# An attention and SwiGLU kernel: new delays between the steps that finish a phase's outputs, a later load of values, and the last projection tile moved among the closing steps

## The chip, the cores and the metric

The kernel runs on one core of a Trainium2 chip. The core has five engines, each with its own queue of instructions that it works through in order: PE multiplies matrices, DVE does vector work, ACT does exponentials and copies, POOL does slower vector work, and SP here only issues transfers (DMAs). Engines wait for each other through semaphores. The metric is device microseconds (us) of one execution, the median of several runs.

## What is computed

The input x has 2048 tokens of width 512. After a layer norm it goes through two branches, both in float32:

```python
xn = _layernorm(x, axis=-1)
qkv = xn @ wqkv                       # 32 heads of 16
p = softmax(q @ k.T * 16 ** -0.5)     # 2048 x 2048 per head
s = concat(p @ v) @ wo
g = silu((silu(xn @ w1) * (xn @ w3)) @ w2)   # inner width 1792
return x + s * g
```

## The kernel before, in words

**Products.** A float32 matrix is split into a high and a low part (`hi`, `lo`), and a product is three matmuls (`split3`, lines 187, 189 and 191; in the feed-forward branch line 814).

**Phases.** Attention goes by 32 phases: 16 pairs of heads, each with two halves of the queries. For a phase, PE makes scores keys by queries (`scores`, line 587, tile `e`), ACT exponentiates them (line 590, tile `pt`), and PE multiplies the result with the values (`values`, line 600, tile `pv`), in 16 steps over the keys, each called a V step below and numbered through the kernel from 0 to 511. The score matmul also subtracts a maximum of each query's row, which rides along as two extra rows of `qs`. These maxima come from a second pass of scores, queries by keys (`max_unit`, line 380, tile `m`), reduced by DVE (line 382, tile `mp`). When a phase's maxima are complete, `max_rows` works in three stages: DVE reduces and negates (lines 388 and 390), PE transposes and DVE splits into `mh` and `ml` (394 to 398), and SP issues four transfers that write the rows into `qs` (line 405). The next phase's `e` matmuls wait for them.

**A phase's outputs.** After a phase's last V step, `take_out` copies `pv` to `ot` at once (ACT, line 606) and then goes on in six steps, called *sums* (4 transfers of the softmax's sums, line 612), *reciprocal* (DVE, 614), *rd* (1 transfer of the reciprocals to memory, 616), *rb* (4 transfers that read them back spread over rows, 619), *multiply* (DVE 621, then the split `oh`, `ol` on POOL, 624 and 625), and *out* (8 transfers, 633). The list `outs` holds the phases whose steps are still to come.

**What orders the work.** Nothing is decided on the chip. A planner in the Python code keeps a clock (`mod.now`) that it advances by fixed costs, and emits instructions as it goes; each engine then runs its own in that order. A long string, `ORDER_OF_ISSUE`, says what PE gets next: s and S are score matmuls of one half of the array's rows, m and M maxima, f and F the feed-forward branch, v a V step, r and R the middle stage of `max_rows`, o a tile of the output projection, a dot a pause. Before every character the planner calls `settle`, `small` (which takes the steps of `max_rows` and `take_out` that are due), `tend` (transfers of the last part, `tasks`) and `catch_up` (characters that could not be served when they came, the list `late`; it serves several o's in a row with no call of `small` between them).

In `small`, before, each output step is due a fixed time of the planner's clock after the last: 7.0, and 4.0 for phases from 27 on:

```python
if c[0] <= mod.now:
    c[0] = mod.now + (7.0 if c[2] < PHASES - 5 else 4.0)
```

**The last part.** `steps` lists 22 pieces of the output projection. A piece ("whole", b, t), called tile (b, t) below, is 12 matmuls, for a block b of 512 tokens and t of its four 128-token tiles; blocks go in the order 3, 2, 0, then the rest of block 2, then 1. `finish` multiplies by the gate, adds x (lines 983 and 984) and stores. Tiles (0, t) and (1, t) need the outputs of phase 30, which `taken_out(PHASES - 2)` asks for; its *out* step writes straight into the tiles `ov` that they read (k = 3 of each product, the last three of 12 matmuls). When block 2's tiles are issued, `tend` issues eight loads for block 1 (lines 914 and 915, 256 KB each) into the space that block 2 frees; those of block 0 go the same way before. Phase 31 ends with a closing stretch of its own (lines 1226 to 1245): ACT copies `pv` (1227), the remaining tiles are run, `shares` sums with PE and takes reciprocals (1032 to 1035), `turn_back` transposes (1041), DVE multiplies (1238), ACT and DVE split (1240, 1241), and four last products follow.

Of the kernel before, what the change touches and what calls it, by code (L numbers as in the profile page):

```python
# [1 line left out]

# [14 lines left out]
P = 128  # L17
S, D, F = 2048, 512, 1792
H, DH = 32, 16
NP = H // 2  # L20
KC = D // P
# [13 lines left out]
GH = 4  # L35
RING = 9
AHEAD = 5
HALF = P // 2
EARLY = 0.5

# [86 lines left out]
    "svvSmMmsMvSsMmvSffMSfMfSffMfMfSfFfFsFsFmFsFfFmFsFfMsFfFmFsFfMfSfFsFmMfFfSfFfSmFfFmFsSfFmSvvvmSmSsFFs"  # L129
    "FmFFsFmFFsmFmFFsFmFmFsFFmFsFmFsSvSmFsmFsSvvsSsSsSvvmSSsSsvvmSsSsSSvmSsSSvvMsSsSsMvMsMsMsvMsMsMsS...."  # L130
    "..oSssSSrSovSssSSsSovvSssSSsosSsSSsvvsSsSSovsSSsSovSsSsSovSsSvvvoooooSssSSsosSvsSsSosSvvSsoooooosSSs"
    "SsosSsSSsovsvsvvv..."
)


def raw(ap):
    return ap.bitcast(F32)
# [3 lines left out]
def kernel(ctx: ExitStack, tc: tile.TileContext, x, wqkv, wo, w1, w3, w2, out):  # L141
    nc = tc.nc
# [14 lines left out]
    def take(v):  # L157

        i = min(range(BANKS), key=lambda i: (free_at[i], taken_at[i]))
        uses[i] += 1  # L160
        kind[i] = v
        was_free[i] = free_at[i]
        taken_at[i] = sum(uses)
        free_at[i] = max(t for t in free_at if t < 1e8) + 0.001
        return i, psum.tile([P, 512], F32, tag=f"bank{i}", name=v, bufs=1)

    def bank(v):
        return take(v)[1]
# [16 lines left out]
    def split3(ps, lhs, rhs, first, last):  # L185

        nc.tensor.matmul(ps, lhs[1], rhs[0], start=first, stop=False)  # L187
        yield
        nc.tensor.matmul(ps, lhs[0], rhs[1], start=False, stop=False)  # L189
        yield  # L190
        nc.tensor.matmul(ps, lhs[0], rhs[0], start=False, stop=last)  # L191
        yield

    def run(gen):
        for _ in gen:
            pass
# [90 lines left out]
    mod = Model()  # L287
# [120 lines left out]
    with tc.tile_pool(name="pro", bufs=1) as pro:  # L408
# [24 lines left out]
        half = pro.tile([P, 1], F32, name="half")  # L433
# [88 lines left out]
        for b in range(TB):  # L522
# [4 lines left out]
            for i, u in enumerate((2, 3, 0, 1) if b == 0 else (2, 0, 1, 3)):  # L527
                t = b * 4 + i

                for v in range(2):  # L530
                    rbk = u * 2 + v
                    ps = bank("e")
# [26 lines left out]
                r = next(blank, None)  # L559
# [84 lines left out]
    def settle():  # L644
        wts.fill()
        for e in list(owed):
            if e in owed and e[0] <= max(mod.now, mod.free[e[1]] if e[1] in mod.free else 0) + 0.1:
                owed.remove(e)
                e[3](e[0])
# [188 lines left out]
    ov, wos, side, sums, there = {}, [], {}, [], {}  # L838
# [113 lines left out]
    def tend():  # L952

        while tasks and not any(c[2] for c in rows) and mod.free["dma"] <= mod.now + 3.0:
            e = next((e for e in tasks if e[1]()), None)
            if e is None:
                return
            tasks.remove(e)
            e[2]()
            if e[3]:  # L960
                there[e[0]] = mod.work("dma", mod.now, e[3]) + 2.5
# [5 lines left out]
    steps = [("whole", b, t) for b in (3, 2, 0) for t in range(4)]  # L967
# [11 lines left out]
    def finish(b, t, i, ps, to, adder=None):  # L979

        xr, gr = side[b, t]
        res = tail.tile([P, 512], F32, tag="res", name="res", bufs=2) if adder is None else pt_tile(F32)
        nc.vector.scalar_tensor_tensor(res, gr, 0.25, ps, op0=ALU.mult, op1=ALU.mult)
        (adder or nc.vector).tensor_add(xr, res, xr)
        free_at[i] = mod.work("dve", max(mod.lane) + 0.25, 1.4) - 0.7
        if to is not None:
            r = b * 512 + t * P
            to.dma_start(out[r:r + P, :], xr)

    def pt_tile(dtype):  # L990
        return work.tile([P, 512], dtype, tag="pt", name="pt", bufs=PTS)

    def projecting():

        if not steps or min(free_at) > mod.now + EARLY or not can(*steps[0][:2]):
            return False
        what, b, t = steps.pop(0)
        i, ps = take("o")
        if what == "sum":
            mod.block(3, was_free[i])  # L1000
            side["spread"] = shares(sums[0], ps, tail.tile([P, 512], F32, tag="res", name="res", bufs=2))
            free_at[i] = mod.work("dve", max(mod.lane) + 0.25, 0.8) - 0.5
            sums.append(free_at[i] + 0.8)
            return True
        if what == "back":
            mod.block(4, was_free[i])
            ot = sums[0]
            turn_back(ps, side["spread"])
            oh, ol = (work.tile([P, 512], F32R, tag=f"o{v}", name=f"o{v}", bufs=1) for v in "hl")
            nc.vector.tensor_mul(ot, ot, ps)  # L1010
            nc.vector.tensor_scalar(oh, ot, 1.0, 1.0, op0=ALU.mult, op1=ALU.mult)
            nc.vector.tensor_sub(ol, ot, raw(oh))
            free_at[i] = mod.work("dve", max(mod.lane) + 0.25, 2.0) - 1.2
            sums.append(free_at[i] + 1.5)
            side["split"] = oh, ol
            return True
        if what == "whole":
            mod.block(3 * KC, was_free[i])
            for k in range(KC):
                run(split3(ps, [v[k][:, t * P:(t + 1) * P] for v in ov[b]], [w[k] for w in wos], k == 0, k == KC - 1))  # L1020
        else:
            mod.block(3, was_free[i])
            run(split3(ps, [v[:, t * P:(t + 1) * P] for v in side["split"]], wlast, True, True))
        finish(b, t, i, ps, nc.sync if b < TB // 2 or what == "last" else None)
        return True
# [3 lines left out]
    def shares(ot, ps, spread):  # L1029

        for c in range(4):
            nc.tensor.matmul(ps[:, 4 * c:4 * c + 4], ot[:, c * P:(c + 1) * P], picks[0], start=True, stop=True)
        rec = work.tile([P, 16], F32, tag="rec", name="rec", bufs=2)
        nc.vector.reciprocal(rec, ps[:, 0:16])
        nc.vector.tensor_copy(spread.rearrange("p (a b) -> p a b", b=32),
                              rec.rearrange("p (a b) -> p a b", b=1).to_broadcast([P, 16, 32]))
        return spread

    def turn_back(ps, spread):
        for c in range(4):  # L1040
            nc.tensor.transpose(ps[:, c * P:(c + 1) * P], spread[:, c * P:(c + 1) * P], ident)
# [66 lines left out]
    def small(due=False):  # L1108

        for c in list(rows):  # L1110
            if c[2] == 1 and not due or c[2] != 1 and c[0] > mod.now:
                continue
            if c[2] == 0:
                c[0] = mod.work("dve", mod.now, 0.4) + 1.5
            if next(c[1], "end") == "end":
                ready[c[3]] = mod.free["dve"] + 3.5
                rows.remove(c)
            elif c[2] == 1:
                c[0] = mod.now
            c[2] += 1  # L1120
        for c in list(outs):
            if c[0] <= mod.now:
                c[0] = mod.now + (7.0 if c[2] < PHASES - 5 else 4.0)
                if next(c[1], "end") == "end":
                    outs.remove(c)

# [7 lines left out]
    def issue_v():  # L1134
        nonlocal pv_free
        c = closed.pop(0)
        p, half, k = c["at"]
        there = max(c["end"], pv_free if fresh(c["at"]) else 0.0)
        values(p, half, k, [c["pts"][j] for j in range(4)])
        if k == half == 0 and 2 * p % GH == 0 and 0 < 2 * p < H - GH:  # L1140
            load_v(2 * p // GH + 1)
        begins = mod.whole(mod.VALUES, there)
        multiplied[count["V"]] = begins + mod.VALUES + 0.2
        state["seen"] = max(state["seen"], c["last"])
        count["V"] += 1
        if (p, half) == LAST:
            if k == NT // 2 - 1:
                sums.append(work.tile([P, 512], F32, tag="ot", name="ot", bufs=2))
                nc.scalar.copy(sums[0], pv)
                pv_free = mod.work("act", begins + mod.VALUES + 0.3, 0.6) + mod.NOTICE  # L1150
                sums.append(pv_free)
        elif k == NT - 1:
            g = take_out(p, half)
            next(g)
            pv_free = mod.work("act", begins + mod.VALUES + 0.3, 0.6) + mod.NOTICE
            outs.append([mod.now + 2.0, g, p * 2 + half])

    def half_issued(what, h):

# [65 lines left out]

    ot, oh, ol = pt_tile(F32), pt_tile(F32R), pt_tile(F32R)
    nc.scalar.copy(ot, pv)
    while steps:
        settle()
        small()  # L1230
        tend()
        mod.wait(0.1)
        projecting()
    spread, back = shares(ot, bank("o"), pt_tile(F32)), bank("o")
    turn_back(back, spread)
    halves = slice(0, 256), slice(256, 512)
    for c in halves:
        nc.vector.tensor_mul(ot[:, c], ot[:, c], back[:, c])
    for c in halves:
        nc.scalar.copy(oh[:, c], ot[:, c])  # L1240
        nc.vector.tensor_sub(ol[:, c], ot[:, c], raw(oh[:, c]))
    for t in range(4):
        i, ps = take("o")
        run(split3(ps, [v[:, t * P:(t + 1) * P] for v in (oh, ol)], wlast, True, True))
        finish(3, t, i, ps, nc.scalar if t % 2 else nc.sync, nc.gpsimd if t < 2 else nc.vector)
# [27 lines left out]
```

## Time and profile before

| | |
|---|---|
| runs before | 1798.92, 1799.48, 1799.76 us; median 1799.48 |
| profiled execution | 1797.59 us, of which the span from first to last instruction is 1795.5 |
| PE busy | 1760.3 us, 98% of the span |
| DVE busy | 1479.3 us, 82% |
| ACT busy | 1246.9 us, 69% |
| POOL busy | 698.1 us, 39% |
| transfers | 155.64 MB, nearly all in one queue, SP's |

In the timeline, a row has the start, the busy time, engine, line, operation, tiles, and in brackets the engine's idle time before it with what ended it. In the view of waits, a row has who waited for what, total us, times, and the longest. A row "x8" merges eight instructions that follow each other.

### The profile page before, as it was taken

Reading aid. Unit: us, or ns where it says so; the run is one execution under the profiler, and the core shown is the slowest. Engines: PE = TensorE matmul, PEld = TensorE weight load, DVE = VectorE, ACT = ScalarE, POOL = GpSimd, SP = SyncE. Lnnn points to the kernel's source line nnn. Section 1 sums busy time; section 2 is a strip of 40 time slices with the busy share of each in tenths; the row PEclk is TensorE's granted clock in tenths of the full one; section 3 lists DMA queues with packets and bytes.
Section 4 is the critical chain, followed back from the end, with each engine's and each line's share of the span. In section 5 each row is a group of like instructions: output and inputs, shape, how many; then the busy total and the mean of one; then the engine's idle time right before and its main releaser. Section 6 shows DMA issues by size and latency. Waiting matters only on the chain.

```text
span 1795.5 us, 35452 instructions
## 1 busy us (share of the span) xinstructions
PE 1760.3 (98%) x13136; PEld 1041.5 (58%) x13136; DVE 1479.3 (82%) x2466; ACT 1246.9 (69%) x2360; POOL 698.1 (39%) x730
## 2 busy tenths in 40 slices
PE   7999999999999999999899999999999999999998
PEld 6766555555565555555455565556555555555455
DVE  6666998888998998988788889888988998899525
ACT  3222787777777787787677777878768777777861
POOL 2101546055605462445325542555056605552100
PEclk9999999999999999999999999999999999999999
DMA  7646313041323212231422230233223212132552
GB/s 256 242 179 191 84 37 84 20 92 50 75 87 85 58 49 54 57 83 46 112 66 64 55 72 19 68 81 106 52 72 82 61 37 60 40 72 84 158 184 94
DMA packets 147724, 155.64 MB, mean 87 GB/s; under 512 B 43104, under 2 KB 101472, under 8 KB 144576
## 3 DMA queue, kind: packets, MB, share of 16 engines
q1 hardware_dynamic: 147264, 152.86, 30.7%
q8 instruction: 103, 1.69, 0.4%
q14 instruction: 69, 0.57, 0.1%
q10 hardware_dynamic: 288, 0.52, 0.1%
HBM read 108.23 MB, written 44.03 MB: 85 GB/s over the span
## 4 chain that ended last, share of the span: by engine, by line
PE 93%; DVE 3%; DMA 1%; POOL 1%; issue 1%; SPq 1%; ACT 0%; DVEq 0%; POOLq 0%; ACTq 0%
PE pv L600 26%; PE f L814 25%; PE e L587 17%; PE m L380 14%; DVE mp L382 2%; PE e L187 2%; PE e L191 2%; PE e L189 2%; PE o L187 1%; PE m L187 1%; PE o L189 1%; PE o L191 1%; PE m L189 1%; PE m L191 1%; DMA xtl<-xt 1%
## 5 line engine op out<-in xcount | busy, mean ns | idle before, releaser
L382 DVE TENSOR_REDUCE mp<-m 128x1 f32<-128x512 f32 x2048 | 1298.5, 683 | 168.0 <-PE m L380 99.7
L590 ACT ACTIVATE pt<-e 128x512 f32<-128x512 f32 x2048 | 1090.1, 606 | 342.9 <-PE m L380 148.0
L587 PE MATMUL e<-qs,ks 64*128 64x512 f32 x2048 | 732.2, 417 | 4.3 <-DMA qs<-ml 3.9
L380 PE MATMUL m<-ks,qs 62*128 62x512 f32 x2048 | 698.0, 414 | 9.6 <-DVE mp L382 6.0
L600 PE MATMUL pv<-pt,vt 128*17 128x512 f32 x4096 | 515.9, 596 | 0.0
L587 PEld LDWEIGHTS e<-qs,ks 64*128 64x128 f32 x2048 | 347.8, 185 | 288.5 <-ACT pt L590 103.7
L380 PEld LDWEIGHTS m<-ks,qs 62*128 62x128 f32 x2048 | 336.0, 185 | 130.8 <-DVE mp L382 43.1
L600 PEld LDWEIGHTS pv<-pt,vt 128*17 128x17 f32 x4096 | 83.9, 96 | 203.0 <-issue 190.2
L814 PE MATMUL f<-xth,wl 64*128 64x512 f32 x488 | 173.7, 396 | 0.2 <-DVE mp L382 0.2
L814 PE MATMUL f<-xth,wh 64*128 64x512 f32 x488 | 173.3, 393 | 0.0
L814 PE MATMUL f<-xtl,wh 64*128 64x512 f32 x488 | 172.9, 394 | 0.0
L624 POOL TENSOR_SCALAR oh<-ot 128x512 fp32r<-128x512 f32 x31 | 19.2, 620 | 354.4 <-DVE ot L621 343.7
L814 PE MATMUL f<-wh,hs 64*128 64x512 f32 x496 | 154.5, 395 | 0.0
L700 POOL TENSOR_TENSOR h<-g,h 128x512 f32<-128x512 f32 x56 | 71.9, 1284 | 195.8 <-ACT h L696 192.4
L814 PE MATMUL f<-xth,xel 64*128 64x512 f32 x408 | 147.4, 398 | 0.1
L814 PE MATMUL f<-xth,xeh 64*128 64x512 f32 x408 | 146.6, 394 | 0.0
L814 PE MATMUL f<-xtl,xeh 64*128 64x512 f32 x408 | 146.5, 395 | 0.0
L814 PE MATMUL f<-xeh,hs 64*128 64x512 f32 x400 | 126.1, 394 | 1.6 <-POOL hs L702 1.6
L313 POOL TENSOR_TENSOR wl<-wr,wh 128x512 fp32r<-128x512 f32 x92 | 118.5, 1288 | 7.7
L313 POOL TENSOR_TENSOR xel<-wr,xeh 128x512 fp32r<-128x512 f32 x76 | 98.3, 1294 | 6.3
L814 PE MATMUL f<-wl,hs 64*128 64x512 f32 x248 | 91.9, 397 | 0.0
L312 POOL TENSOR_SCALAR wh<-wr 128x512 fp32r<-128x512 f32 x92 | 57.2, 622 | 88.2 <-PE e L587 54.5
(173 smaller groups left out, 2022.2 us busy)
## 6 DMA issues: line engine op xcount, KB each, us to landing
wr<-in_B_w_dram SPq DMA_DIRECT2D x168, 256.0 KB
qs<-qk SPq DMA_DIRECT2D x186, 64.0 KB
ks<-qk SPq DMA_DIRECT2D x90, 128.0 KB
qk<-sh SPq DMA_DIRECT2D x32, 256.0 KB
qk<-sl SPq DMA_DIRECT2D x32, 256.0 KB
v<-vrow SPq DMA_DIRECT2D x16, 272.0 KB
xin<-in_A_x_dram SPq DMA_DIRECT2D x16, 256.0 KB
g<-part SPq DMA_DIRECT2D x16, 256.0 KB
```

What stands on the lines that cost most here:

```text
L187: nc.tensor.matmul(ps, lhs[1], rhs[0], start=first, stop=False)
L189: nc.tensor.matmul(ps, lhs[0], rhs[1], start=False, stop=False)
L191: nc.tensor.matmul(ps, lhs[0], rhs[0], start=False, stop=last)
L312: nc.gpsimd.tensor_scalar(hi, t, 1.0, 1.0, op0=ALU.mult, op1=ALU.mult)
L313: nc.gpsimd.tensor_sub(lo, t, raw(hi))
L380: nc.tensor.matmul(ps, qs[p % 2][64 * h:64 * h + KM, q0:q0 + P], ks[p % 2][64 * h:64 * h + KM, c * 512:(c + 1) * 512], start=True, stop=True)
L382: nc.vector.reduce_max(mp[p, half][:, h, qt, c:c + 1], ps, axis=AX.X)
L587: nc.tensor.matmul(ps, ks[p % 2][64 * h:64 * h + KR, k * P:(k + 1) * P], qs[p % 2][64 * h:64 * h + KR, q0:q0 + 512], start=True, stop=True)
L590: nc.scalar.activation(pt, ps, AF.Exp, scale=DH ** -0.5)
L600: nc.tensor.matmul(pv[32 * j:32 * j + VW, :], vt[2 * p // GH][:, key, 2 * p % GH + j % 2, :], pt, start=key < 2 if last else k == 0, stop= ...
L700: nc.gpsimd.tensor_mul(h2, g, h2)
L814: nc.tensor.matmul(ps, left[r], right[r], start=starts and lane == 0, stop=ends and lane == 1)
```

## The change

- The output steps get delays of their own. `LATER` (phases 0 to 26) and `SOON` (27 to 30) give the planner's time after step 0 to 5; each phase's entry in `outs` has a counter for it.
- An output step is not taken while a `max_rows` is between its first stage and its last.
- The load of the next group's values is issued with the V step k = 10 of a phase, not k = 0.
- One o is gone from the order's end, so that one projection tile, (1, 3), is left when the string is done; in the closing stretch its 12 matmuls are cut in 4, 3 and 5 around `shares` and `turn_back`, and its `finish` comes behind the splits, with the add on POOL and the store in ACT's queue.

```diff
+LATER = (12.0, 1.5, 8.0, 12.0, 5.0, 0.0)
+SOON = (5.0, 1.5, 4.0, 5.0, 3.0, 0.0)
...
-    "SsosSsSSsovsvsvvv..."
+    "SsosSsSsvsSsvvvv.."
...
+    def products(b, t, ps):
+        for k in range(KC):
+            yield from split3(ps, [v[k][:, t * P:(t + 1) * P] for v in ov[b]], [w[k] for w in wos], k == 0, k == KC - 1)
...
         for c in list(outs):
-            if c[0] <= mod.now:
-                c[0] = mod.now + (7.0 if c[2] < PHASES - 5 else 4.0)
+
+            if c[0] <= mod.now and not any(r[2] for r in rows):
+                c[3] += 1
+                c[0] = mod.now + (LATER if c[2] < PHASES - 5 else SOON)[c[3]]
                 if next(c[1], "end") == "end":
                     outs.remove(c)
...
-        if k == half == 0 and 2 * p % GH == 0 and 0 < 2 * p < H - GH:
+        if half == 0 and k == 10 and 2 * p % GH == 0 and 0 < 2 * p < H - GH:
             load_v(2 * p // GH + 1)
...
-            outs.append([mod.now + 2.0, g, p * 2 + half])
+            outs.append([mod.now + 2.0, g, p * 2 + half, -1])
...
     nc.scalar.copy(ot, pv)
-    while steps:
-        settle()
-        small()
-        tend()
-        mod.wait(0.1)
-        projecting()
+    _, b, t = steps.pop()
+    i, ps = take("o")
+    rest = products(b, t, ps)
+    run(islice(rest, 4))
     spread, back = shares(ot, bank("o"), pt_tile(F32)), bank("o")
+    run(islice(rest, 3))
     turn_back(back, spread)
+    run(rest)
     halves = slice(0, 256), slice(256, 512)
     for c in halves:
         nc.vector.tensor_mul(ot[:, c], ot[:, c], back[:, c])
     for c in halves:
         nc.scalar.copy(oh[:, c], ot[:, c])
         nc.vector.tensor_sub(ol[:, c], ot[:, c], raw(oh[:, c]))
+    finish(b, t, i, ps, nc.scalar, nc.gpsimd)
```

More of the change, by code (lines that the diff above doesn't have):

```diff
@@ L1 @@
 from contextlib import ExitStack
+from itertools import islice
 import concourse.bass as bass
@@ L1018, in projecting @@
             mod.block(3 * KC, was_free[i])
-            for k in range(KC):
-                run(split3(ps, [v[k][:, t * P:(t + 1) * P] for v in ov[b]], [w[k] for w in wos], k == 0, k == KC - 1))
+            run(products(b, t, ps))
         else:
```

## The prediction

> **What bounds the kernel now.** I read the page first, then PE's waits, then the timeline around the longest of them, then the end. The page says that PE is busy nearly throughout, so that only PE's idle time, or a slow clock, can be won back.
>
> ```profile
> span 1795.5 us, 35452 instructions
> PE 1760.3 (98%) x13136; PEld 1041.5 (58%) x13136; DVE 1479.3 (82%) x2466; ACT 1246.9 (69%) x2360; POOL 698.1 (39%) x730
> ```
>
> PE's waits (who for whom: us, times, longest), without those of the first stretch, which the change leaves alone:
>
> ```profile
> PE m L380 <- DVE mp L382: 6.0, 4, 5.1
> PE e L587 <- DMA qs<-ml: 3.9, 2, 3.6
> PE f L814 <- POOL hs L702: 1.6, 2, 1.3
> PE o L187 <- DVE pt L1241: 1.5, 1, 1.5
> PE o L1041 <- DVE pt L1035: 0.9, 1, 0.9
> PE o L1032 <- ACT pt L1227: 0.8, 1, 0.8
> ```
>
> So there are two long stalls, 5.1 and 3.6 us, and three short ones that all stand at the very end. The first long one, from DVE, PE and SP:
>
> ```profile
> 882.38 0.68 DVE L724 TENSOR_TENSOR part<-part,f 128x512 f32<-128x512 f32 x1
> 890.72 0.25 DVE L614 RECIPROCAL rec<-sums 128x16 f32<-128x16 f32 x1 [7.67 <-DMA sums<-ot]
> ...
> 886.61 0.49 PE L587 MATMUL e<-qs,ks 64*128 64x512 f32 x1
> 892.17 0.79 PE L380 MATMUL m<-ks,qs 62*128 62x512 f32 x1 [5.07 <-DVE mp L382]
> ...
> 883.50 5.96 SPq L612 DMA_DIRECT2D sums<-ot  x4
> ```
>
> DVE comes to a phase's reciprocal at 883.06 and stands there for 7.67 us, because SP was late with the *sums* transfers. Behind it in DVE's queue stand the maxima; with none of their banks freed, PE lasts until 887.10, 4.0 us, and then stands for 5.07.
>
> The second long one, from SP and PE:
>
> ```profile
> 1309.04 0.38 SPq L298 DMA_DIRECT2D wr<-in_B_w_dram  x1
> 1309.47 0.49 SPq L633 DMA_DIRECT2D o<-oh  x1
> ...
> 1312.80 0.42 SPq L633 DMA_DIRECT2D o<-ol  x1
> 1313.31 0.72 SPq L405 DMA_DIRECT2D qs<-mh  x1
> ...
> 1315.51 0.63 SPq L405 DMA_DIRECT2D qs<-ml  x1
> ...
> 1313.15 0.61 PE L600 MATMUL pv<-pt,vt 128*17 128x512 f32 x4
> 1317.36 0.47 PE L587 MATMUL e<-qs,ks 64*128 64x512 f32 x1 [3.59 <-DMA qs<-ml]
> ```
>
> Here the eight *out* transfers of an older phase go ahead of the four rows of maxima. SP spends 1309.47 to 1313.31, 3.84 us, on them; the last row is written 1.2 us after its issue has ended, and PE has been waiting since 1313.77.
>
> Each of the long stalls, and the end, is followed by a stretch at half clock (a row: stretch, its length, busy time and count of PE, weight loads, DVE, ACT and POOL, then the granted clock, the share of the DMA engines and GB/s):
>
> ```profile
> 891.90:895.30 3.40, 3.13 (x14) 3.03 (x16) 2.60 (x5) 1.19 (x2) 0.00 (x0) 0.50 0.23 80
> 1318.60:1321.90 3.30, 3.30 (x18) 2.91 (x16) 2.48 (x4) 2.02 (x4) 0.00 (x0) 0.50 0.96 268
> 1786.20:1789.50 3.30, 3.30 (x9) 2.60 (x8) 1.38 (x2) 0.00 (x0) 1.50 (x2) 0.50 0.00 0
> ```
>
> Some 3.4 us at 0.50 do the work of 1.7. A long stall thus costs 1.7 us more than its idle time.
>
> **The delays of the output steps.** No instruction is added. DVE's reciprocal comes 12.0 us of the planner's clock behind *sums*. It was to come 7.0 behind, but a step is taken at the next character, and at this place that made 7.8. So it moves by 4.2 us, DVE would wait 7.67 - 4.2 = 3.5, and PE lasts 4.0 without DVE: the idle 5.07 goes, and the 1.7 with it. **Minus 6.8**; bounds 0 (another step is late in its place) and 6.8. Late next is *multiply*, which waits for *rb*; it gets 12.0 instead of 7.0.
>
> *rd* comes 1.5 behind the reciprocal, not 7.0: SP then waits for DVE now and then, with weight loads behind it, which have four buffers. *out* comes 5.0 behind *multiply*, not 7.0; POOL's split ends 2.1 us after *multiply* (below, 1741.54 to 1743.62), so SP waits only where POOL is behind with weights. Both are 0 with that cover; without it a load is late by a few us, and what that costs is bounded by a stall like the one at 1317, 5.3.
>
> *multiply* and POOL's split come some 5 us later than now. POOL's split can then stand before an `hs` that PE waits for, or no longer stand there: plus or minus the 1.3 us of the table of waits. I take 0.
>
> **The rows first.** With the new condition the eight *out* transfers at 1309.47 can't come between. The rows, whose values I take as ready (SP goes over to them without a pause), then start 3.84 us earlier, and the wait that ended at 1317.36 would end at 1313.52, before PE's 1313.77. **Minus 3.59 - 1.7 = minus 5.3**; bounds 0 and 5.3. What was held comes behind the rows, so a phase's steps end later. Their delays add to 2.0 + 12.0 + 1.5 + 8.0 + 12.0 + 5.0 = 40.5 us, and a held step can add some 8; a phase is long enough for that, 1479.1 / 30 = 49.3 us by the copies of `pv`:
>
> ```profile
> L606 ACT COPY ot<-pv x31: 586/587/620, 233.2 to 1712.3; 128x512 f32<-128x512 f32 x31
> ```
>
> **The load of values at k = 10.** Seven, less the first, of 544 KB. It leaves the place just ahead of *sums* and comes near the rows of the next phase. PE waits for neither of them there now, so 0; bounds plus and minus 3.6, the one long wait for rows.
>
> **The closing stretch.** Now:
>
> ```profile
> 1776.26 0.39 PE L187 MATMUL o<-ks,xel 128*128 128x512 f32 x1
> ...
> 1779.08 1.91 PE L600 MATMUL pv<-pt,vt 128*17 128x512 f32 x16
> 1781.75 1.05 PE L1032 MATMUL o<-picks,pt 128*128 128x4 f32 x8 [0.76 <-ACT pt L1227]
> 1783.68 0.66 PE L1041 MATMUL o<-ident,pt 128*128 128x128 f32 x4 [0.88 <-DVE pt L1035]
> 1785.82 0.52 PE L187 MATMUL o<-wh,pt 128*128 128x512 f32 x1 [1.48 <-DVE pt L1241]
> ...
> 1791.81 0.69 DVE L984 TENSOR_TENSOR wr<-pt,wr 128x512 f32<-128x512 f32 x1
> ```
>
> From the last V step's end (1780.99) to the last add's end (1792.50) pass 11.5 us. The change takes tile (1, 3), 1776.26 to 1779.08, from ahead of the V steps: they end 2.8 earlier. Its 12 matmuls, 0.23 each, fill the gaps. Counted from the V steps' end: four matmuls to 1.0, the sums of shares as now 1.05 long, so the transposes begin at 1.0 + (1783.68 - 1781.75) = 2.9, the first closing product at 2.9 + (1785.82 - 1783.68) = 5.1, all four at full clock end at 5.1 + 12 x 0.23 = 7.9. DVE is then the bound: after the splits, at 5.4, it has five multiplies and two adds of 0.69, to 10.2. That is 1.3 under 11.5, with PE never idle long enough to lose its clock. Sum 2.8 + 1.3 = 4.1; one more store of 256 KB among the last, taken as 0.2. **Minus 3.9**; bounds 2.6 (half clock again) and 4.1.
>
> **Phase 30's steps, and what they set free.** This is where the change can lose. `SOON` makes these steps *earlier* in the order. Worked through the order with the delays: *rd* falls before V step 499, *rb* before 502, *multiply* behind the tiles (2, 1) to (2, 3), which run with no step taken between, and *out* right behind V step 504. Before, *rb* was behind those tiles, *multiply* before 505 and *out* after 506. Tile (0, 0) waits in `late` for *out* to be issued, so it now follows V step 504 instead of 506, though nothing makes its data earlier:
>
> ```profile
> 1739.52 0.35 SPq L914 DMA_DIRECT2D inh<-in_A_x_dram  x1
> ...
> 1743.29 0.53 SPq L633 DMA_DIRECT2D ovh<-oh  x1
> ...
> 1745.66 0.51 SPq L633 DMA_DIRECT2D ovl<-ol  x1
> ...
> 1740.86 0.68 DVE L621 TENSOR_TENSOR ot<-ot,rb 128x512 f32<-128x512 f32 x1
> ...
> 1742.34 1.28 POOL L625 TENSOR_TENSOR ol<-ot,oh 128x512 fp32r<-128x512 f32 x1
> ...
> 1741.09 1.53 PE L600 MATMUL pv<-pt,vt 128*17 128x512 f32 x8
> 1742.55 1.49 PE L587 MATMUL e<-qs,ks 64*128 64x512 f32 x6
> ...
> 1747.37 0.50 PE L187 MATMUL o<-ks,ovl 128*128 128x512 f32 x1
> ...
> 1749.54 0.39 PE L187 MATMUL o<-ks,ovl 128*128 128x512 f32 x1
> ...
> L187 PEldq EVENT_SEMAPHORE  x1: 411/411/411, 1748.8 to 1748.8; - x1
> ```
>
> *multiply* stands behind the adds of tile (2, 3) in DVE's queue in both, and SP issues the eight loads of block 1 (from 1739.52) ahead of *out* in both. The last of the four transfers for block 0 goes out at 1745.66, and PE's queue waited for it 0.41 us from 1748.8: it landed at about 1749.2, just in time for the tenth matmul at 1749.54. In the new order the tile starts where the V step ends, about 1742.1 (two V steps take 1.91), its tenth matmul is due 2.2 later, at 1744.3, and waits until 1749.2: 4.9 us idle, in place of 12 `e` matmuls and two V steps, which now come later. They took 5.2 us, some of it waiting; I take 4.7. With half clock behind it, 1.7: **plus 6.4**; bounds 0 (the data come earlier, too) and 6.9. At this place the Trainium skill, "TensorE: Matmul & The Clock Gate", Part 1, speaks for less: the clock falls after at least one idle window of about 3.4 us. An idle time of 4.9 need not hold a whole free-running window, and the sum would be 1.7 lower. The trace goes against so strict a reading: 3.59 us idle sufficed at 1317, and at the end no idle time was over 1.48.
>
> **The sum.** -6.8 - 5.3 - 3.9 + 6.4 = -9.6. The profiled execution took 1797.59 us (span 1795.5 and 2.1 around it) and would take 1788.0; the median before is 1799.48, 1.9 above that execution, so **1789.9 us**.
>
> **Rivals.**
> - *No new wait at tile (0, 0)*: the planner's steps shift *out* and tile together. For it: PE has no such wait now. Against: the 0.41 us say that the tile is already as early as its data. -16.0: 1783.5.
> - *The wait, but no half clock behind it*, by the skill's rule above, worked out here as an idle time of 4.9 us that fills no window and costs no 1.7. For it: the end had half clock with other idle times, so the rows don't say what sets it off. Against: both long stalls had it. -11.3, 1788.2.
> - *One long stall stays or comes back elsewhere* (a step lands on other late transfers; 27 phases are shifted, and two of them stalled before): one of 5.3 to 6.8 stays, 1795 to 1797.
> - *The change does not do what it says*: both long stalls only move, the end and the new wait remain: -3.9 + 6.4 = +2.5, 1802.0.
> - *Slower*: the longer chain's *out* meets the next phase's *sums* in SP's queue (40.5 to 48 us against 49.3 on average). SP waits for POOL's split, spends 3.84 us on eight issues, and *sums* come late enough for DVE to stand as at 883, 6.8 each time. For it: both stand in one queue. Against: *sums* now have 12.0 us. It decides from two such places on: -9.6 + 13.6 = +4.0, 1803.5, with three 1810.
>
> **How the numbers follow.** Forecast 0.45 (1787 to 1793), without half clock 0.10, no new wait 0.14, a stall stays 0.16, only moved 0.07, slower 0.08. The range from 1782.5 to 1797 leaves out the last two cases and little of the others. A measurement of this kernel tells 0.2%, 3.6 us, from no change: faster, below 1795.9, holds the first three and half of the fourth, 0.77; same 0.15; slower 0.08.
>
> **What would show it.** Right: no wait of `rec` for `sums` over 4 us and no PE wait for `mp` over 1; no PE wait for `qs<-ml` over 1; the three short waits at the end under 0.5 each and no half clock there; a new PE wait of an `o` matmul of about 4.9 us for `ov` from *out*, between V steps 504 and 505, with 3.4 us at 0.50 behind it. Wrong: a new wait in the 27 phases with `LATER`, above all for `sums`, or the transfers of `ov` landing before tile (0, 0) asks for them.

## The result, and the profile after

The changed kernel takes 1805.25 us (median of 7 runs, 1801.61 to 1807.19). The kernel before, run beside it, takes 1800.05 us (7 runs, 1798.92 to 1803.01). The ratio is 1.0025, with a 95% interval from 1.0014 to 1.0036: the change makes the kernel 0.25% slower. The prediction was 1789.9, in a range up to 1797.0, so both its value and its sign were wrong.

The profiled execution took 1803.67 us, with a span of 1801.9; the one of before took 1797.59, with a span of 1795.5. That is 6.4 us of span to explain. The page's first lines say again that only PE's idle time and its clock can have done it:

```profile
span 1801.9 us, 35478 instructions
PE 1761.5 (98%) x13136; PEld 1039.7 (58%) x13136; DVE 1480.9 (82%) x2465; ACT 1246.9 (69%) x2360; POOL 701.2 (39%) x731
```

PE's waits of the changed kernel (who for whom: us, times, longest), without those of the first stretch:

```profile
PE m L384 <- DVE mp L386: 12.0, 7, 6.1
...
PE o L191 <- DMA ovl<-ol: 4.1, 1, 4.1
...
PE e L591 <- DVE mp L386: 1.2, 2, 1.0
PE f L818 <- POOL hs L706: 1.0, 2, 0.8
...
PE o L191 <- DVE pt L1250: 0.3, 1, 0.3
```

The wait for `qs<-ml` is gone, and so are the three short waits at the end but for 0.3. The wait for DVE's `mp` has grown from 6.0 to 12.0, and the wait for `ovl` is new. DVE's own waits say that the 12.0 are two stalls of different origin:

```profile
DVE rec L618 <- DMA sums<-ot: 6.5, 1, 6.5
...
DVE ot L625 <- DMA rb<-rd: 5.0, 2, 4.0
```

So the changed kernel has three long stalls where the old one had two. In the timeline they look as follows.

```profile
893.65 0.79 PE L384 MATMUL m<-ks,qs 62*128 62x512 f32 x1 [6.11 <-DVE mp L386]
...
1589.16 0.50 PE L384 MATMUL m<-ks,qs 62*128 62x512 f32 x1 [4.12 <-DVE mp L386]
...
1751.99 0.76 PE L191 MATMUL o<-ks,ovl 128*128 128x512 f32 x1 [4.14 <-DMA ovl<-ol]
```

The first stands where the old stall of 5.07 stood, the second is new and was not foreseen, the third is the wait of tile (0, 0). Windows around them (stretch, length, busy time and count of PE, weight loads, DVE, ACT and POOL, granted clock, share of the DMA engines, GB/s) show half clock behind each, and none in the closing stretch (last row):

```profile
890.30:893.70 3.40, 0.05 (x2) 0.05 (x2) 0.90 (x3) 0.00 (x0) 0.00 (x0) 0.51 0.23 80
893.70:897.10 3.40, 3.40 (x16) 2.71 (x18) 2.32 (x4) 1.22 (x3) 0.00 (x0) 0.50 0.03 4
1590.10:1593.50 3.40, 3.40 (x20) 1.43 (x20) 2.77 (x5) 2.13 (x4) 1.00 (x2) 0.50 0.24 54
1750.60:1754.00 3.40, 2.01 (x5) 1.65 (x6) 0.35 (x1) 0.00 (x0) 0.00 (x0) 0.50 0.16 36
1754.00:1757.30 3.30, 3.30 (x10) 2.53 (x9) 1.02 (x2) 0.00 (x0) 0.00 (x0) 0.50 0.21 79
1790.00:1793.40 3.40, 2.99 (x14) 1.92 (x15) 2.30 (x7) 0.73 (x2) 0.00 (x0) 1.00 0.02 5
```

Half clock costs only what PE works in it, halved. The stretch that begins at 890.3 is idle until 893.65, so it costs (897.1 - 893.65) / 2 = 1.7; the one at 1590 costs 1.7; the one at 1750.6, where PE goes on at 1751.99, costs (1757.3 - 1751.99) / 2 = 2.7.

The account of the span, after less before:

| place (idle time plus half clock) | us |
|---|---|
| 892: 6.11 + 1.7 in place of 5.07 + 1.6 | +1.1 |
| 1317: 3.59 + 1.7, gone | -5.3 |
| 1589, new: 4.12 + 1.7 | +5.8 |
| 1752, new: 4.14 + 2.7 | +6.8 |
| closing stretch (the run below) | -3.6 |
| `hs`: 0.8 in place of 1.3; two new short waits for `mp`, 1.0 and 0.7 | +1.2 |
| sum | +6.0 |

The span grew by 6.4. The starts of the V steps, after less before, bear out the long rows: the difference grows by 1.0 from V step 224 to 228 (the stall at 892), falls by 5.0 from 364 to 366, grows by 5.6 from 452 to 454 and by 4.1 from 504 to 511, where the changed kernel has 2.8 us of work less in between. From 366 to 452 it also grows by 2.5 in small steps, of which the table has 1.0.

### The profile page after: what moved, and what is told of

It is laid out like the page before. It is cut to its first block, busy times and chain, and to the rows that moved or that the text cites. A ratio compares the mean times of both kernels' runs of the same rounds, so it can differ in the third digit from the quotient of the medians.

```text
span 1801.9 us, 35478 instructions
## 1 busy us (share of the span) xinstructions
PE 1761.5 (98%) x13136; PEld 1039.7 (58%) x13136; DVE 1480.9 (82%) x2465; ACT 1246.9 (69%) x2360; POOL 701.2 (39%) x731
## 4 chain that ended last, share of the span: by engine, by line
PE 89%; DVE 4%; DMA 3%; issue 2%; POOL 1%; SPq 1%; ACT 1%; DVEq 0%; POOLq 0%; ACTq 0%
PE pv L604 25%; PE f L818 24%; PE e L591 16%; PE m L384 13%; DVE mp L386 2%; PE e L191 2%; PE e L195 1%; PE e L193 1%; PE m L191 1%; PE m L193 1%; PE m L195 1%; DMA xtl<-xt 1%; PE o L191 1%; DVE ot L625 1%; PE o L193 1%
## 5 line engine op out<-in xcount | busy, mean ns | idle before, releaser
L688 POOL TENSOR_SCALAR th<-th 128x512 f32<-128x512 f32 x56 | 34.7, 620 | 152.9 <-ACT th L681 152.9
```

## The experiments

The kernel before ran beside each of the kernels below on the same chip, and each ratio is to that. A difference to the changed kernel is the ratio less 1.0025, times 1800 us; the interval of each of the two ratios is about plus and minus 2 us, that of the difference some 3.

### The parts that should gain, each alone on the kernel before

The closing stretch alone (with the string's end):

```diff
-    "SsosSsSSsovsvsvvv..."
+    "SsosSsSsvsSsvvvv.."
...
-    while steps:
...
+    run(islice(rest, 4))
     spread, back = shares(ot, bank("o"), pt_tile(F32)), bank("o")
+    run(islice(rest, 3))
     turn_back(back, spread)
+    run(rest)
```

> The kernel before with the closing stretch of the change alone. By the prediction's step: 3.9 us faster than before (bounds 2.6 to 4.1), with the three short waits at the end under 0.5 us each. Rival, that tile (1, 3) only changes its place and the net is what the changed kernel's end shows (3.4 us gained from tile (2, 3) to the end): 3.4. Rival, that the gain exists only where phase 30's outputs come at another time: under 1 us.

Measured: 1796.27 us, ratio 0.9980 (0.9972 to 0.9989), 3.6 us faster. In its profile only one of the three short waits is left, 0.3 long. The step of the prediction (3.9, bounds 2.6 to 4.1) holds.

The hold for the maxima's rows alone:

```diff
-            if c[0] <= mod.now:
+            if c[0] <= mod.now and not any(r[2] for r in rows):
```

> The kernel before with the condition that holds an output step while the maxima's rows are between their stages, and the old delays of 7.0 and 4.0. By the prediction's step: the wait for qs<-ml at 1317 and the half clock behind it are gone, 5.3 us faster, and the long stall at 892 stays. Rival, that the held steps themselves make new late transfers, as the stall that the changed kernel has at 1589 behind the outputs of phase 26 that were held: that stall shows here too, 4 us idle and some 1.7 of half clock, and the sum is 0 (plus or minus 1).

Measured: 1794.18 us, ratio 0.9966 (0.9953 to 0.9979), 6.1 us faster. PE has no wait for `qs<-ml` at 1317 (V steps 364 to 366 take 5.0 us less), the stall at 892 stays (5.4 us here), and at 1589 there is none: the longest PE gap between 1560 and 1690 is 0.12. So the step holds, and the hold by itself does not make the new stall.

The load of values at k = 10 alone:

```diff
-        if k == half == 0 and 2 * p % GH == 0 and 0 < 2 * p < H - GH:
+        if half == 0 and k == 10 and 2 * p % GH == 0 and 0 < 2 * p < H - GH:
```

> The kernel before with the load of the next values at k = 10 instead of k = 0, nothing else. By the prediction's step: no difference (bounds plus and minus 3.6, one long wait for rows); both long stalls stay. Rival, that it is what makes the rows later (it goes out close behind them): PE waits for qs<-ml more than 3.9 us in all and the kernel is 2 us or more slower.

Measured: 1797.85 us, ratio 0.9995 (0.9986 to 1.0004). Nothing that a run can tell from no change, as predicted; both old stalls stay, and PE's wait for rows is the same 3.9 us.

### The wait of tile (0, 0)

Phase 30 alone back on the old delay:

```diff
-                c[0] = mod.now + (LATER if c[2] < PHASES - 5 else SOON)[c[3]]
+                c[0] = mod.now + (LATER if c[2] < PHASES - 5 else SOON if c[2] < PHASES - 2 else [4.0] * 6)[c[3]]
```

> The changed kernel, phase 30 alone with the old delay of 4.0. Theory (the wait of tile (0, 0) is made by phase 30's earlier steps): PE's wait of o for ovl is gone and the half clock of 6.8 us at 1750 with it, 6 to 7.5 us faster than the changed kernel; all ahead of 1690 is as in the changed kernel, the stall at 1588 too. Rival, that the tile is as early as its data in any order (the string, not the delays, sets it): the wait shrinks by under 2 us and the time by as little.

Measured: 1798.48 us, ratio 0.9991 (0.9982 to 0.9999), 6.1 us faster than the changed kernel. PE has no wait for `ovl` left. In this order two more V steps and twelve more `e` stand ahead of tile (0, 0); its tenth matmul comes at 1755.12, 0.4 us after the ninth, and the last *ovl* had gone out at 1750.91. The wait belongs to phase 30's earlier steps, as the prediction had it.

All of phases 27 to 30 back on 4.0:

```diff
-SOON = (5.0, 1.5, 4.0, 5.0, 3.0, 0.0)
+SOON = (4.0, 4.0, 4.0, 4.0, 4.0, 0.0)
```

> The changed kernel, phases 27 to 30 with the old delay of 4.0 throughout. Theory: both new stalls of the changed kernel (multiply waiting for rb at 1588, PE idle 4.1 and half clock; tile (0, 0) waiting for ovl, 4.1 and half clock) come from SOON: both gone, 11 to 13 us faster than the changed kernel, some 1792 to 1794. Rival, that the stall at 1588 is made by the held outputs of phase 26 ahead of phase 27's transfers, not by SOON: it stays, only the wait at tile (0, 0) goes, 6 to 7.5 us faster than the changed kernel, some 1798.

Measured: 1797.16 us, ratio 0.9988 (0.9979 to 0.9996), 6.7 us faster than the changed kernel. By this time alone, that is what phase 30 gives, and not the 11 to 13 of the theory that `SOON` makes both new stalls. The theory fell by half: the stall at 1589 seems to have another cause.

### The stall at 1589

SP's queue there, in the changed kernel:

```profile
1565.44 2.46 SPq L616 DMA_DIRECT2D sums<-ot  x4
1568.01 0.53 SPq L637 DMA_DIRECT2D o<-oh  x1
...
1571.37 0.42 SPq L637 DMA_DIRECT2D o<-ol  x1
1571.88 3.96 SPq L363 DMA_DIRECT2D ks<-qk  x6
...
1576.35 4.20 SPq L372 DMA_DIRECT2D qs<-qk  x6
1581.05 0.34 SPq L620 DMA_DIRECT2D rd<-rec  x1
```

The eight *out* transfers here are phase 26's, on `LATER` and therefore late; around them stand the steps of phase 27, which is on `SOON`. The first phase of the short chain meets the last of the long one. Its *rd* goes out at 1581.05 although the reciprocal was done at 1571.7. The chain of waits (start, us, what) then runs without a break to PE:

```profile
1581.05 3.31 DMA rd<-rec
...
1585.66 1.86 DMA rb<-rd
...
1587.81 0.69 DVE ot L625
...
1589.16 0.50 PE m L384
```

The test is to put phase 26 alone back on 7.0:

```diff
-                c[0] = mod.now + (LATER if c[2] < PHASES - 5 else SOON)[c[3]]
+                c[0] = mod.now + (LATER if c[2] < PHASES - 6 else [7.0] * 6 if c[2] < PHASES - 5 else SOON)[c[3]]
```

> The changed kernel, phase 26 alone with the old delay of 7.0. Theory: the stall at 1588 is made where the long chain of LATER meets the short one of SOON: the eight out transfers of phase 26 (1568.0 to 1571.8) stand in SP's queue behind the sums of phase 27 and ahead of its rd and rb, and phase 27's multiply comes at its short delay. With phase 26 on 7.0 its out transfers go ahead of these sums, the wait of multiply for rb (4.0) and PE's idle time (4.1) are gone with the half clock behind them: 4 to 6 us faster than the changed kernel, 1799 to 1801. Rival, that SOON alone makes it (multiply 15.5 us of the planner's clock behind sums, with two ks and qs loads between): it stays, the time is that of the changed kernel, 1805.

Measured: 1798.60 us, ratio 0.9996 (0.9988 to 1.0005), 5.2 us faster than the changed kernel. The same place in this kernel's SP queue, and DVE's *multiply*, which now waits for nothing:

```profile
1562.04 0.42 SPq L637 DMA_DIRECT2D o<-ol  x1
1565.53 2.47 SPq L616 DMA_DIRECT2D sums<-ot  x4
1568.10 2.84 SPq L363 DMA_DIRECT2D ks<-qk  x6
...
1576.67 0.34 SPq L620 DMA_DIRECT2D rd<-rec  x1
...
1583.09 0.68 DVE L625 TENSOR_TENSOR ot<-ot,rb 128x512 f32<-128x512 f32 x1
```

*sums* go out at the same time, *rd* 4.4 us earlier. Up to V step 448 the two traces agree within 0.7 us, and at 454 this one is 6.3 ahead. So the stall comes of phase 26's delays, which put its *out* between phase 27's *sums* and *rd*; the hold alone, on the old delays, does not make it.

### The stall at 892

The reciprocal was moved, and yet the stall is longer. DVE in the changed kernel:

```profile
880.26 0.68 DVE L728 TENSOR_TENSOR part<-part,f 128x512 f32<-128x512 f32 x1
...
883.17 3.16 DVE L386 TENSOR_REDUCE mp<-m 128x1 f32<-128x512 f32 x5 [0.82 <-PE m L384]
892.80 0.25 DVE L618 RECIPROCAL rec<-sums 128x16 f32<-128x16 f32 x1 [6.46 <-DMA sums<-ot]
```

Before, the reciprocal stood right behind the add of line 724 (here 728). Now a multiply-add and five reductions stand between, so that DVE comes to it at 886.34 and not at 880.94: 5.4 us later in its own work. By the clock of the two traces it is 3.3 later (883.06 before), because the work here runs 2.1 us ahead (V step 224 starts at 879.9, before at 882.0).

What DVE waits for is seen in SP's waits between 884 and 893 of the changed kernel, and in the same place before, between 883 and 892:

```profile
SPq L616 <- DMA xtl<-xt: 4.7, 1, 4.7
SPq L616 <- DMA xth<-xt: 2.2, 1, 2.2
```

```profile
SPq L612 <- DMA xtl<-xt: 3.6, 1, 3.6
SPq L612 <- DMA xth<-xt: 2.2, 1, 2.2
```

SP stops between the four *sums* transfers until a load of x, 1 MB each half, has landed. The load is issued 0.9 us later than before by the clock, and takes 1.2 us longer to land, so the last *sums* come 2.1 later, which is 4.2 later against DVE's and PE's work. The chain of waits names the load as most of the way, first before, then in the changed kernel:

```profile
876.17 11.46 DMA xtl<-xt
```

```profile
877.05 12.66 DMA xtl<-xt
...
890.94 1.74 DMA sums<-ot
```

Why SP holds these two transfers can be counted off its queue: in the trace its transfers tell of their landing on eight semaphores in turn. Between the halves of the load and *sums* stand six loads of `qs`, so the first *sums* is the eighth transfer behind `xth` and the second the eighth behind `xtl`. In the changed kernel's trace 60 of the 74 waits of SP for a landing are for the transfer eight places back; the other 14 are for data that the transfer itself reads (`rb` for `rd`, `ks` for `qk`). Where the eight *out* follow the load directly, as in the kernel with the hold alone, it is the seventh and eighth of them that wait for `xth` and `xtl`, 2.2 us each.

Why the load goes out later was not separated. Ahead of it SP waits 3.8 and 1.0 us for POOL's split of an older phase's outputs, and then 0.4 us for PE; before, the *out* transfers there waited for nothing.

If the load is the cause, its place is enough to remove the stall. The second load of x goes out one tile of the feed-forward branch later:

```diff
-                    if t == 1 and hf == 1 and n + 1 < TB:
+                    if t == 1 + (n == 1) and hf == 1 and n + 1 < TB:
```

> The changed kernel, where the second of the three loads of x (two transfers, 2 MB) is issued one tile of the feed-forward branch later, which puts it behind the four sums transfers of phase 13 instead of ahead of them. Theory: the stall at 892 stands on these loads, since SP waits for them (a second sums transfer goes out only at 890, when xtl lands) and they fill the transfer engines. Without them the sums go out in 2.5 us and land at about 888.5, the reciprocal waits under 2.5 us, PE under 1, and the half clock of 6.8 us goes too: 6.1 + 3.4 = 9.5 us less the rest, 8 to 9.5 faster than the changed kernel, 1796 to 1797.5. Rival, that rd and rb, now behind these loads, come late in their turn: multiply of phase 13 waits for rb, and the gain is under 4 us.

Measured: 1797.41 us, ratio 0.9988 (0.9979 to 0.9996), 6.7 us faster than the changed kernel; between V steps 192 and 228 the trace gains 8.0. The *sums* take 3.29 us to issue in place of 7.08, and the reciprocal does not wait. No stall of PE comes from *rb* behind the load. The whole kernel gains less than the 8 to 9.5 expected, because 1.8 us are lost again at the other new stall, between V steps 452 and 456: there PE is idle for 4.6 us and not 4.1, and half clock lasts 6.8 and not 3.4.

The other way is to move the reciprocal further, in phase 13 alone. SP's order is then the same in every row:

```diff
-                c[0] = mod.now + (LATER if c[2] < PHASES - 5 else SOON)[c[3]]
+                c[0] = mod.now + ((18.0, 1.5, 6.0, 8.0, 5.0, 0.0) if c[2] == 13 else LATER if c[2] < PHASES - 5 else SOON)[c[3]]
```

> The changed kernel, phase 13 alone with the delays (18, 1.5, 6, 8, 5, 0): SP's order is the same in every row, DVE comes to this one reciprocal nine reductions and one add later (9 x 0.62 + 0.68 = 6.3 us). Theory, that the step was right and too small: DVE reaches it at 886.3 + 6.3 = 892.6, about when the sums land (892.7); its wait is under 1 us, PE's 6.1 and the half clock behind it go, 7 to 8.5 us faster than the changed kernel, 1797 to 1798. Rival, that PE stands for the sums' lateness in another way (its rows or the next multiply): under 3 us.

Measured: 1796.61 us, ratio 0.9986 (0.9977 to 0.9994), 7.0 us faster than the changed kernel. SP still takes 7.00 us over the *sums*, but DVE is busy through it and PE has no gap there:

```profile
885.67 7.00 SPq L616 DMA_DIRECT2D sums<-ot  x4
...
894.52 0.24 DVE L618 RECIPROCAL rec<-sums 128x16 f32<-128x16 f32 x1
```

And the move undone, again in phase 13 alone, with (7.0, 1.5, 8.0, 17.0, 5.0, 0.0) in the same place:

> The changed kernel, phase 13 alone with the delays (7, 1.5, 8, 17, 5, 0): the reciprocal stands ahead of five reductions and a multiply-add again, as before the change, and ahead of the V steps on PE from 882.6 to 884.5. DVE stops at 880.9 and the sums land at 892.7, a wait of 11.7. Theory, that PE's cover is made of the V steps and the free banks that happen to stand behind the reciprocal, not a time that goes along with it: three maxima and two groups of V steps still run, PE stops at 884.9, 4.0 us after DVE (1.2 in the changed kernel), idle 8 to 9 us: 2 to 3 us slower than the changed kernel, although DVE stands 5.2 longer. Rival, that PE's own order at this place has lost the cover: PE stops 1.2 us after DVE, idle over 10.5, 5 us slower.

Measured: 1808.35 us, ratio 1.0048 (1.0035 to 1.0060), 4.1 us slower than the changed kernel.

```profile
881.58 0.68 DVE L728 TENSOR_TENSOR part<-part,f 128x512 f32<-128x512 f32 x1
893.59 0.25 DVE L618 RECIPROCAL rec<-sums 128x16 f32<-128x16 f32 x1 [11.33 <-DMA sums<-ot]
...
884.80 1.05 PE L604 MATMUL pv<-pt,vt 128*17 128x512 f32 x8
885.79 0.49 PE L591 MATMUL e<-qs,ks 64*128 64x512 f32 x1
895.04 0.79 PE L384 MATMUL m<-ks,qs 62*128 62x512 f32 x1 [8.76 <-DVE mp L386]
```

DVE stops at 882.26 and PE at 886.28: the 4.0 us of cover are back. In the changed kernel DVE stopped at 886.34 and PE at 887.54, 1.2 us later. So the cover is the V steps, and the few `e` and `m` between them, that PE still has to do when DVE stops. A reciprocal moved past them leaves them behind: it came 5.4 us later in DVE's work, and PE got only 2.6 us further in its own (7.6 us from the start of V step 224 to the stop, against 5.1 in this run and before the change). The idle time came out as expected (8 to 9). The time did not (4.1 slower, not 2 to 3), because the half clock lasted longer: it held from 891.0 to 901.2, of which PE worked 6.2 us, 3.1 lost and not 1.7.

### The reciprocal later in all phases, and versions that beat both

```diff
-LATER = (12.0, 1.5, 8.0, 12.0, 5.0, 0.0)
+LATER = (18.0, 1.5, 6.0, 8.0, 5.0, 0.0)
```

> The changed kernel with LATER = (18, 1.5, 6, 8, 5, 0), the same sum, so that the reciprocal comes 6 us of the planner's clock later still (11 reductions later in DVE's queue at the first place where the orders differ). Theory, that the step was right and only too small: the sums land at 891.5, DVE would come to the reciprocal 6 us later than at 886.3, so the wait of 6.5 and PE's idle 6.1 go, with half clock 8 to 9.5 us faster than the changed kernel. Rival (what is late next): rd, rb and multiply come behind it in less time, multiply waits for rb in at least one phase with PE idle 3 us or more, and the gain is under 5 us or none.

Measured: 1790.08 us, ratio 0.9949 (0.9937 to 0.9961), 13.7 us faster than the changed kernel. That is more than expected. Between V steps 222 and 228, where the stall was, it gains 7.6; the rest gathers in small steps (3.9 us ahead of V step 222, 3.3 behind 228), and only some 1.8 of them are seen as waits that are gone (for `hs` 0.8 at 683, for `mp` 1.0 at 1512). The feared new wait did not come; the stalls at 1575 (4.1) and at tile (0, 0) (5.1) are the old ones.

From the parts that gain, on the kernel before with its old delays (closing stretch, hold, and the second load of x one tile later):

> The kernel before with the closing stretch, the condition for the rows, and the second load of x one feed-forward tile later; the old delays. By the runs so far: 3.5 from the closing stretch, 6.1 from the rows first; and from the load of x 6.8 if the stall at 892 goes (sums landed some 888, reciprocal waits under 3). Sum 16.4 faster than before: 1783, from 1781 to 1786, faster than either kernel. Rival, that the stall stays or moves to multiply: 1789 to 1791.

Measured: 1783.23 us, ratio 0.9911 (0.9898 to 0.9924), 16.0 us faster than before. The three gains add up.

And the change itself, with its faults mended by delays alone:

```diff
-LATER = (12.0, 1.5, 8.0, 12.0, 5.0, 0.0)
+LATER = (18.0, 1.5, 6.0, 8.0, 5.0, 0.0)
...
-                c[0] = mod.now + (LATER if c[2] < PHASES - 5 else SOON)[c[3]]
+                c[0] = mod.now + (LATER if c[2] < PHASES - 6 else [7.0] * 6 if c[2] < PHASES - 5 else SOON if c[2] < PHASES - 2 else [4.0] * 6)[c[3]]
```

> The changed kernel with the three faults that the runs so far name mended by delays alone: LATER = (18, 1.5, 6, 8, 5, 0), phase 26 on the old 7.0 and phase 30 on the old 4.0. If the causes are separate, it is the 1790.1 of the kernel with the later reciprocal, less the stall of multiply at 1575 there (4.1 idle and 1.7 of half clock, 5.8) and the wait of tile (0, 0) (5.1 and 1.6, 6.7): 1777.6, from 1776 to 1780, faster than every kernel so far. Rival, that one stall comes back in another phase: 1783 to 1785.

Measured: 1777.36 us, ratio 0.9875 (0.9862 to 0.9889), 22.5 us faster than before and 27 faster than the changed kernel. Its longest PE waits behind the first stretch (to some 180 us):

```profile
PE m L384 <- DVE mp L386: 1.4, 3, 0.7
PE e L591 <- DVE mp L386: 0.4, 1, 0.4
```

No long stall is left, and it came out where the sum of the single causes put it (1777.6). They are separate causes, then. The later reciprocal brought more than the stall at 892 cost, as said above, and what the rest of its gain is made of stays open.

## Why the prediction was wrong

**The first long stall: the step that failed.** The prediction said: "So it moves by 4.2 us, DVE would wait 7.67 - 4.2 = 3.5, and PE lasts 4.0 without DVE: the idle 5.07 goes, and the 1.7 with it. Minus 6.8". It measured plus 1.1 in the trace. The move was larger than computed, 5.4 us of DVE's work and not 4.2. But both numbers it was set against changed with the order. The *sums* landed 4.2 us later against that work, so that DVE still waited 7.67 - 5.4 + 4.2 = 6.5: they hang on the load of x, whose place and landing the prediction had not looked at, though SP's 5.96 us for four *sums* transfers stood in its own fence. And PE's 4.0 us were V steps at a fixed place in PE's order, past which the reciprocal was moved. Either alone would have spoilt the gain, by an estimate from these rows: PE goes on 0.85 us after the reciprocal starts (892.80 to 893.65), so a wait of 3.5 with a cover of 1.2 leaves some 3.2 us idle, and a wait of 6.5 with a cover of 4.0 some 3.3. That 0.85 was left out of the sum too: a wait of 3.5 and a cover of 4.0 leave some 0.4 idle and not none. The idea itself was sound but too small; 6 us more in phase 13 removed the stall.

**The delays of the output steps, taken as 0.** This failed too. The new stall at 1589 cost 5.8 in the trace and 5.2 by the run without it. The prediction had given this a bound ("a stall like the one at 1317, 5.3"), and named a new wait in the phases with `LATER` as what would prove it wrong. Its rival "slower" told the mechanism nearly right: a longer chain's *out* meets the next phase's steps in SP's queue. Two details were off. *out* came behind *sums* and ahead of *rd*, so that not the reciprocal but *multiply* was late; and it happened once, at the seam from `LATER` to `SOON`, where a chain of 40.5 us is followed by one of 20.5 in all. The prediction worked its order through for phase 30 and never for the seam. It also took as 0 that SP would wait for POOL's split; SP does so ahead of the load of x (3.8 and 1.0 us), and what that adds to the first stall is not known.

**Tile (0, 0): right.** Predicted plus 6.4 (4.9 idle of which 4.7 is work not done in its place, and half clock), measured 6.1 by the run and 6.8 in the trace. The mechanism is as told, but the number is partly luck, since two misses cancel: the wait was 4.1 and not 4.9, the half clock cost 2.7 and not 1.7. The rival without half clock fell, and so did the one without the wait.

**The rows first: right.** Minus 5.3 predicted, 6.1 measured alone, 5.0 between two V steps.

**The closing stretch: right.** Minus 3.9 predicted, 3.6 measured. From the V steps' end to the last add pass 10.6 us where 10.2 were predicted, since two of the last adds took 0.93 and 1.04 us and not 0.69.

**POOL's split and the load of values: right at 0.** The wait for `hs` is 0.8 in place of 1.3, and the load alone changes nothing that can be told.

Put together: -9.6, plus 7.9 for the first stall (plus 1.1 in place of -6.8), plus 5.8 for the seam, gives +4.1. Of the other 2.3 to the span's 6.4, the short waits are 1.2, tile (0, 0) 0.4 and the closing stretch 0.3; 0.4 stays open. The changed kernel has two of the three good parts of the kernel that runs at 1783, and lost all they gave to two stalls of its own making.

## What to carry to other kernels

When an instruction is moved to hide a wait, work out again both ends of that wait in the new order: when the data land, which can hang on a large transfer elsewhere in the queue (here eight places ahead), and what the idle engine still has to do from the new place on. Where two schedules meet, work through the seam, for the last steps of the slow one stand in the queue among the first of the fast one. And a sum with a large gain from a wait's removal is only as good as the name of what ends the wait: the chain of waits gave it here in one row, a load of 1 MB.

## What the runs showed of the hardware

The price of a stall is not fixed, even in the same order. The stall at 892 with the same idle time, 5.07 us, was followed by one stretch at half clock before the change, and covered by two with the closing stretch alone. The windows of the kernel before:

```profile
891.90:895.30 3.40, 3.13 (x14) 3.03 (x16) 2.60 (x5) 1.19 (x2) 0.00 (x0) 0.50 0.23 80
895.30:898.70 3.40, 3.40 (x31) 3.28 (x30) 3.15 (x5) 2.85 (x6) 0.00 (x0) 1.00 0.00 0
```

and of the kernel with the closing stretch alone:

```profile
890.80:894.20 3.40, 1.51 (x7) 1.42 (x9) 2.96 (x6) 0.60 (x1) 0.00 (x0) 0.50 0.23 80
894.20:897.60 3.40, 3.40 (x19) 3.40 (x18) 1.76 (x4) 1.70 (x3) 0.00 (x0) 0.50 0.00 0
```

In the traces such stretches behind a stall were 3.4, 6.8 or (after 8.76 us idle) 10.2 us long. They lie on a grid: within each of the thirteen traces read here, every stretch at half clock begins a whole number of 3.413 us after the first (in the changed kernel the first at 40.44, the later ones 17, 249, 454 and 501 such steps on). Where the grid lies differs between traces. The Trainium skill, "TensorE: Matmul & The Clock Gate", Part 1, says that the clock is set by a free-running window of 3413 ns. The lengths and the grid agree with it. Its condition of at least one idle window does not: in the kernel with the later reciprocal a gap of 1.61 us, in a window where PE was busy for 1.80 of 3.41 us, was followed by half clock, while the mended kernel kept full clock behind 1.70 of idle. First the later reciprocal, its window and the stretch behind it, then two windows of the mended kernel, all but the second row cut along the grid:

```profile
175.81:179.22 3.41, 1.80 (x14) 1.08 (x12) 1.91 (x5) 2.42 (x5) 0.00 (x0) 1.00 0.50 118
179.20:182.60 3.40, 3.37 (x16) 2.94 (x16) 2.46 (x5) 1.95 (x4) 0.38 (x1) 0.50 1.23 280
```

```profile
174.46:177.87 3.41, 2.24 (x15) 1.48 (x14) 2.02 (x4) 0.71 (x2) 0.00 (x0) 1.00 0.65 240
177.87:181.28 3.41, 2.80 (x17) 1.60 (x19) 2.35 (x4) 3.03 (x6) 0.00 (x0) 1.00 0.80 177
```

The first gap lies whole in one window; a border of the grid cuts the second in two. Counted over the thirteen traces from 105 us on, PE's busy time in a window of the grid goes with the clock of the next. At full clock, all 25 windows with 1.3 us or less were followed by half clock, and none of the 6325 with over 2.2 us; of the 17 between, with 1.8 to 2.2, three were. At half clock, the 16 windows with 2.8 us or less were followed by another such window, the 28 with 3.1 or more by full clock. That also separates the two stalls of 5.07 us: the first half-clock stretch had PE busy for 3.13 us in one kernel and 1.51 in the other. These are counts and not a trial, since no run moved a stall along the grid on purpose. For a forecast it means that half clock behind a stall cost between 1.6 and 3.1 us here, by where the stall fell on a grid whose place the traces do not foretell.
